# Early products by rows of x, other exact pairs, and a new order in an attention and two-layer MoE kernel

## The chip, the cores and the metric

One NeuronCore of a Trainium2 chip runs the whole program. The metric is the device time of one launch in microseconds (us); a kernel's time is the median of its runs. The engines are TensorE (PE, its weight loads PEld), VectorE (DVE), ScalarE (ACT), GpSimd (POOL) and SyncE (SP), which here issues the DMAs.

## The reference, cut to what is computed

```python
# attention: q, k, v are (4, 8, 576, 64)
scores = softmax(causal(q @ k.T / 8))          # a /= a.sum(-1) + 1e-9
local = scores @ v
q_p = where(q > 0, q, exp(q) - 1) + 1          # phi
mem_out = (q_p @ M_prev) / (q_p @ z_prev + 1e-6)
x = g * mem_out + (1 - g) * local              # g = sigmoid(beta), per head
# x as 2304 tokens x 512
y = (silu(x @ w_gate) * (x @ w_val)) @ w_out   # 1536 hidden columns
h = y @ w_in                                   # 2048 hidden columns
out = where(h >= 1, h, where(h <= -1, 0, (h + 1) ** 2 / 4)) @ w_out2
```

## The kernel before

**Tiling.** The 32 heads are worked as 16 pairs (4 batches of 4 pairs), pairs 0 to 15 in this text. x stands transposed in DRAM (xs): its 512 columns are four rows of 128, and pair n of a batch writes row n for that batch's 576 tokens. A matmul operand is held as a high and a low part, and a product of two such operands is three matmuls (high by low, low by high, high by high). ScalarE makes the high part (a cast, `split`, "name.hi"), VectorE the low part (a difference, "name.lo"); for v and x the difference is GpSimd's. Some pairs instead multiply in plain fp32 from one copied operand ("exact"), which takes TensorE longer and leaves out the low parts: pairs below EXACT (8) for the last product av (probabilities R by v), below EXACT_Q (2) for the scores s (tiles K and SZ), below EXACT_M (4) for the memory product. In a pair with split scores the parts of K for the second head reach the other half of the partitions by a DMA ("dup", K onto K).

**One pair.** q, k, v are loaded by SP; TensorE transposes k and q; scores s; VectorE takes mask, scale and row minimum (a, mn); ScalarE takes the Exp with the row sum; VectorE turns sums into factors (`scales`, with `over`: one scalar_tensor_tensor and one reciprocal); GpSimd scales the rows of a; TensorE transposes them; copies or splits give R; av ends the pair. Beside it phi goes min (VectorE), Exp (ScalarE), p (VectorE), the norm (GpSimd and VectorE), its transposes PP, and enters av by M. A pair with split operands joins av's two halves (ScalarE copy avt, VectorE sum xf), casts x (`x_hi`), takes the difference (`x_lo`) and stores the row (`x_out`).

**Early products.** While attention runs, twelve weight units (gate and val of the first six hidden tiles) are decoded, and for the token groups 0 to 511, 512 to 1023 and 1024 to 1535 the products with them are done as soon as all their batches are stored (`early_unit`): four rows of x are loaded as xh (`load_x`, four buffers), each unit takes 12 matmuls of 512 columns in one PSUM bank of the three called mm, cut into two halves of two rows (CUTS), then ScalarE copies the bank to gvo and SP stores it to gv. A second stage then loads xb, the same four rows for groups of tokens, first the two groups of batch 3 (384 tokens each), does their gate and val products, decodes more weights (raw to wA and wS to wu on VectorE), and goes on with the rest of the first layer and the second layer.

**What sets the order.** A planner (`Plan`) takes tasks with an engine, a cost, a priority and their dependences, plays them through as a list scheduler, and writes each engine's instructions in the order that comes out; the engines run theirs in order. The priority of an attention task is a number for its pair plus an entry of the table ORDER; EARLY holds those of the twelve weight units, GROUP_AT those of the early products of batches 0 to 2, X_AT those of their xh loads. In the second stage each xb group is loaded at priority 22 plus its number, the first weights are decoded at -20.

## Time and profile before

| | before |
|---|---|
| median of 3 runs | 1140.66 us (1140.23 to 1140.68) |
| the profiled execution | 1140.29 us |
| its span in the trace | 1138.2 us |
| TensorE busy | 1092.1 us, 96% |
| VectorE busy | 752.9 us, 66% |
| ScalarE busy | 551.9 us, 48% |
| GpSimd busy | 234.4 us, 21% |

The profiled execution is one more run of the kernel; its span reaches from its first to its last recorded instruction, and 2.1 us of its time lie around the span. Busy times are those of instructions recorded on an engine; waits, semaphores and DMA issues are not counted as busy. A share over the whole span mixes attention (the first 377 us) with the two layers behind it, so the rows further below are cut by stretches.

### The profile page before, as it was taken

The page shows a single profiled execution, that of the slowest core. Times are in us where ns is not written, and L with a number is a line of the kernel's source. Part 1 is how long each engine was busy: PE and PEld are TensorE (multiplying, and loading weights), DVE is VectorE, ACT ScalarE, POOL GpSimd, SP SyncE. Part 2 cuts the span into 40 slices and gives each one's busy share as a digit, 9 for nine tenths or more (in the row PEclk, how much of TensorE's full clock was granted, in tenths as well). Part 3 has the DMA queues.
Part 4 walks back from the last instruction along what each step waited for, and adds up shares of the span by engine and source line. Part 5 has one row for each costly group of instructions (what it writes and reads, how often), then busy time and mean ns, then how long its engine had stood idle before and what let it go on. Part 6 is the DMA issues. An engine that isn't in the chain of part 4 may idle for free.

```text
span 1138.2 us, 16428 instructions
## 1 busy us (share of the span) xinstructions
PE 1092.1 (96%) x5544; PEld 928.9 (82%) x5544; DVE 752.9 (66%) x1698; ACT 551.9 (48%) x1258; POOL 234.4 (21%) x314
## 2 busy tenths in 40 slices
PE   6688999999999699999999999999999999999998
PEld 4455677888888699888889998888888888899997
DVE  5567977788886487799954458999634343343433
ACT  6568886888896144455433334444222222222222
POOL 5568677458464000000000000000000000000000
PEclk9889999999999899999999999999999999999999
DMA  5545854665632878987545466562210110010000
GB/s 120 145 115 140 241 136 139 188 172 157 197 104 87 286 224 292 349 330 243 165 135 168 126 238 203 169 238 93 70 37 1 44 50 1 24 55 1 28 1 28
DMA packets 148644, 157.59 MB, mean 138 GB/s; under 512 B 70224, under 2 KB 109136, under 8 KB 148560
## 3 DMA queue, kind: packets, MB, share of 16 engines
q1 hardware_dynamic: 148560, 156.54, 44.1%
q8 instruction: 44, 0.72, 0.3%
q14 instruction: 40, 0.33, 0.1%
HBM read 105.78 MB, written 42.47 MB: 130 GB/s over the span
## 4 chain that ended last, share of the span: by engine, by line
PE 74%; DVE 8%; ACT 7%; DMA 4%; issue 3%; POOL 2%; SPq 1%; ACTq 0%; POOLq 0%; DVEq 0%
PE mm L1015 37%; PE acc L1245 26%; PE av L842 5%; ACT a L663 2%; PE s L650 1%; PE t L781 1%; DMA KK<-KK 1%; DMA raw<-in_moe_w_val_dram 1%; PE s L684 1%; DVE t L1209 1%; DVE wA L956 1%; DVE h L1222 1%; DVE t L1215 1%; ACT KK L380 1%; DMA raw<-in_moe_w_out_dram 1%
## 5 line engine op out<-in xcount | busy, mean ns | idle before, releaser
L1015 PE MATMUL mm<-xb,wu 128*128 128x512 f32 (+1 forms) x1968 | 413.2, 365 | 9.0 <-DMA xb<-xs 9.0
L1015 PEld LDWEIGHTS mm<-xb,wu 128*128 128x128 f32 x1968 | 359.6, 189 | 51.6 <-issue 9.4
L1245 PE MATMUL acc<-wu,h 128*128 128x512 f32 x864 | 208.1, 390 | 0.0
L1245 PEld LDWEIGHTS acc<-wu,h 128*128 128x128 f32 x864 | 161.7, 188 | 32.4
L1219 ACT CAST h<-t 128x512 fp32r<-128x512 f32 (+1 forms) x140 | 80.9, 578 | 185.4 <-DVE t L1213 90.0
L1245 PE MATMUL acc<-h,wu 128*128 128x512 f32 (+1 forms) x720 | 152.2, 368 | 1.5 <-DVE h L1222 1.4
L1207 DVE SCALAR_TENSOR_TENSOR t<-t 128x512 f32<-128x512 f32 (+1 forms) x80 | 51.0, 637 | 146.7 <-ACT t L1201 146.7
L1245 PEld LDWEIGHTS acc<-h,wu 128*128 128x128 f32 x720 | 131.0, 188 | 19.2 <-DVE h L1222 2.4
L1222 DVE TENSOR_TENSOR h<-t,h 128x512 fp32r<-128x512 f32 (+1 forms) x140 | 89.1, 636 | 79.3 <-ACT h L1219 78.9
L1201 ACT ACTIVATE t<-mm,half 128x512 f32<-128x512 f32 (+1 forms) x80 | 51.5, 644 | 147.4 <-PE mm L1015 147.1
L1015 PE MATMUL mm<-xh,wu 128*128 128x512 f32 x432 | 114.4, 404 | 0.0
L734 POOL TENSOR_SCALAR a<-a,sum 128x256 f32<-128x256 f32 (+3 forms) x144 | 85.8, 613 | 33.4 <-DVE sum L568 17.4
L1015 PEld LDWEIGHTS mm<-xh,wu 128*128 128x128 f32 x432 | 77.2, 189 | 14.4
L663 ACT ACTIVATE a<-a,mn 128x128 f32<-128x128 f32 (+3 forms) x128 | 71.3, 559 | 8.8 <-DVE mn L656 8.3
L1060 ACT COPY gvo<-mm 128x512 f32<-128x512 f32 (+1 forms) x80 | 43.2, 548 | 56.1 <-PE mm L1015 55.0
L656 DVE CUSTOM_DVE_ANT_0 a<-s,mask 128x128 f32<-128x128 f32 (+3 forms) x128 | 58.9, 482 | 12.8 <-PE s L650 9.8
L923 ACT ACTIVATE wA<-raw 128x512 f32<-128x512 f32 x64 | 43.1, 674 | 48.7 <-DVE wu L963 14.9
L960 ACT CAST wu<-wA 128x512 fp32r<-128x512 f32 x64 | 39.7, 620 | 47.8 <-DVE wA L956 45.7
L650 PE MATMUL s<-KK,SX 128*128 128x512 f32 (+3 forms) x224 | 50.1, 340 | 3.5 <-DMA KK<-KK 1.4
L1213 DVE TENSOR_TENSOR t<-t,mm 128x512 f32<-128x512 f32 (+1 forms) x80 | 50.6, 632 | 2.2
L842 PE MATMUL av<-R,vn 128*64 128x320 f32 (+4 forms) x224 | 51.4, 371 | 0.0
L842 PEld LDWEIGHTS av<-R,vn 128*64 128x64 f32 x224 | 30.5, 142 | 24.9 <-issue 6.4
(132 smaller groups left out, 1394.2 us busy)
## 6 DMA issues: line engine op xcount, KB each, us to landing
raw<-in_moe_w_out_dram SPq DMA_DIRECT2D x28, 512.0 KB, 5.4
gv<-gvo SPq DMA_DIRECT2D x48, 256.0 KB, 4.5
xb<-xs SPq DMA_DIRECT2D x24, 512.0 KB, 6.6
gv<-gv SPq DMA_DIRECT2D x24, 512.0 KB, 6.0
xs<-x SPq DMA_DIRECT2D x16, 576.0 KB, 3.0
raw<-in_moe_w_in_dram SPq DMA_DIRECT2D x16, 512.0 KB, 5.6
KK<-KK SPq DMA_DIRECT2D x28, 288.0 KB, 4.2
raw<-in_moe_w_gate_dram SPq DMA_DIRECT2D x12, 512.0 KB, 4.7
```

What stands on the lines that cost most here:

```text
L650: nc.tensor.matmul(s[:, 0:kl], st["S"][h][:, c * P:(c + 1) * P], st["K"][h][:, j, 0:kl], start=(j == 0), stop=(j == 1))
L656: nc.vector.tensor_tensor_reduce(a, st[f"s{h}{c}"][:, 0:kl], self.mask0[:, 512 - kl:512], -0.125, 3.0e38, ALU.add, ALU.min, mn[:, o:o + 1])
L663: nc.scalar.activation(a, a, AF.Exp, bias=mn[:, o:o + 1], scale=-1.0, accum_out=sm[:, o:o + 1])
L734: nc.gpsimd.tensor_scalar(a, a, r, 1.0, op0=ALU.mult, op1=ALU.mult)
L842: nc.tensor.matmul(o[0:m, c0:c1], l, r, start=(i == 0), stop=(i == len(mms) - 1), skip_group_check=True)
L1015: nc.tensor.matmul(out, kt_of(unit, pw, kt), x[kt][:, px, cols], start=(kt == 0 and i == 0), stop=(kt == KT - 1 and i == 2))
L1201: nc.scalar.activation(s["t"], src[0][0](), AF.Relu, bias=half, scale=0.5)
L1207: nc.vector.scalar_tensor_tensor(s["t"], s["t"], 1.0, s["t"], op0=ALU.min, op1=ALU.mult)
L1213: nc.vector.tensor_max(s["t"], s["t"], src[0][0]())
L1219: nc.scalar.copy(s["h"][:, 0], s["t"])
L1222: nc.vector.tensor_sub(s["h"][:, 1], s["t"], f32(s["h"][:, 0]))
L1245: nc.tensor.matmul(state[m][:, 0:o], l, r, start=(f == 0 and i == 0), stop=(f == F - 1 and i == 2), skip_group_check=True)
```

## The change

Nine things change.

1. **Exact pairs.** av is multiplied in fp32 for pairs 0 to 3 only (before 0 to 7); the scores for pairs 0 to 3 (before 0 and 1).
2. **Early products by rows.** A unit's 12 matmuls are cut into four quarters, one for each row of x, and a quarter depends on its own xh row alone (before on all four). An xh load depends on the store of its own row alone.
3. **min by ScalarE.** VectorE's min(q, 0) becomes ScalarE's Relu(-q), and the Exp behind it takes scale -1.
4. **Sums.** The row sums stand in the first column of a tile of two columns whose second column holds 1e-9; a reduction over the two replaces the scalar_tensor_tensor. 1/OGP (the factor of 1 - g) is worked out once, and GpSimd's scaling takes it as its second scalar in place of the constant 1.
5. **Own stores.** The gv stores of the last two hidden tiles of group 1024 to 1535 (four) are issued by ScalarE.
6. **xb loads first.** The first two groups of the second stage have their loads at priority -50 and -49, ahead of the weight decoding at -20.
7. to 9. ORDER, EARLY, GROUP_AT and X_AT have new numbers.

```diff
-EXACT = 8
-EXACT_Q = 2
+EXACT = 4
+EXACT_Q = 4
 EXACT_M = 4
...
-CUTS = (0, 2, 4)
-EARLY = (370, 1555, 928, 1016, 176, 628, 40, 285, 537, 6951, 2735, 393)
+CUTS = (0, 1, 2, 3, 4)
+EARLY = (-442.191, 1095.2181, 3514.6201, 5388.5521, -113.2042, 1597.6845, 2014.1923, 166.5095, 4349.2967, 5245.9815, 1051.2236, -130.0942)
 XH, GVO = 4, 3
+OWN = 2
...
-GROUP_AT, X_AT = (27859, 18087, 4829), (572, 439, -332)
+GROUP_AT, X_AT = (25118.8269, 36624.3422, 30122.3043), (360.7705, 632.4816, -116.8892)
...
 ORDER = {
-    "load": -667, "load_v": -340, "load_z": -340, "load_M": -296, "tk": 12, "tm": -870, "tk.hi": 1965, "tm.hi":
+    "load": -945.7389, "load_v": 592.0326, "load_z": -927.2927, "load_M": -295.3806, "tk": -367.2275, "tm":
...
+        nc.vector.reciprocal(self.OGP, self.OGP)
+
+        self.sum = [ac.tile([P, 9, 2], F32, name=f"sum_{i}") for i in range(3)]
+        for t in self.sum:
+            nc.gpsimd.memset(t[:, :, 1], 1e-9)
...
         def f_min():
             e = st["e"] = self.ph.tile([P, 9, D], F32, name="e", tag="e")
-            nc.vector.tensor_scalar(e, st["qn"], 0.0, None, op0=ALU.min)
+            nc.scalar.activation(e, st["qn"], AF.Relu, scale=-1.0)
 
         def f_exp():
-            nc.scalar.activation(st["e"], st["e"], AF.Exp)
+            nc.scalar.activation(st["e"], st["e"], AF.Exp, scale=-1.0)
...
-        t = add("DVE", c_dve(576), "min", f_min, [l_q], [i_q, i_e], True)
+        t = add("ACT", c_act(576) + 40, "min", f_min, [l_q], [i_q, i_e])
...
-                            "sum": self.sm.tile([P, 9], F32, name="sum", tag="sum")}
+                            "sum": self.sum[i_mn.slot],
+                            "r": self.sm.tile([P, 9], F32, name="r", tag="r")}
...
-                    nc.scalar.activation(a, a, AF.Exp, bias=mn[:, o:o + 1], scale=-1.0, accum_out=sm[:, o:o + 1])
+                    nc.scalar.activation(a, a, AF.Exp, bias=mn[:, o:o + 1], scale=-1.0, accum_out=sm[:, o, 0:1])
...
-            return over(lambda: mk_mn()[1][:, lo:hi], 1e-9, self.OGP[:, n, lo:hi], f"sum{h}",
-                        [t_exp[x] for x in keys], [i_mn])
+            def f_sum():
+                mk_mn()
+                nc.vector.tensor_reduce(st["mn"]["r"][:, lo:hi], st["mn"]["sum"][:, lo:hi], axis=AX.X, op=ALU.add)
+
+            def f_inv():
+                r = st["mn"]["r"][:, lo:hi]
+                nc.vector.reciprocal(r, r)
+
+            t = add("DVE", 80, f"sum{h}", f_sum, [t_exp[x] for x in keys], [i_mn])
+            return add("DVE", 94, f"sum{h}", f_inv, [t], [i_mn])
...
-                r = mk_mn()[1][:, o:o + 1]
-                nc.gpsimd.tensor_scalar(a, a, r, 1.0, op0=ALU.mult, op1=ALU.mult)
+                nc.gpsimd.tensor_scalar(a, a, st["mn"]["r"][:, o:o + 1], self.OGP[:, n, o:o + 1], op0=ALU.mult, op1=ALU.mult)
...
-    def early_unit(plan, mm, f, tok, x, pool, prio, tag, cap, deps=()):
+    def early_unit(plan, mm, f, tok, x, pool, prio, tag, cap, deps=(), own=False):
...
-                t = [plan.add("PE", cost, prio - (i > 0), lambda i=i, prod=prod: prod(i), t + [u["t"], *x["t"], *deps],
-                              [i_p, u["i"], *x["i"]])]
+                t = [plan.add("PE", cost, prio - (i > 0), lambda i=i, prod=prod: prod(i),
+                              t + [u["t"], *x["t"][CUTS[i]:CUTS[i + 1]], *deps],
+                              [i_p, u["i"], *x["i"][CUTS[i]:CUTS[i + 1]]])]
             t = plan.add("ACT", c_act(gt), prio - 1, copy, t, [i_p, i_o])
-            plan.dma(prio, [1.42 * gt], lambda j=j: nc.sync.dma_start(gv[f][:, j, tok], s["o", j]), [t], [i_o])
+            if own:
+                t = plan.add("ACT", 50, prio - 2, lambda j=j: nc.scalar.dma_start(gv[f][:, j, tok], s["o", j]), [t], [i_o])
+                plan.add("DMA", 1.42 * gt, prio, lambda: None, [t], [i_o])
+            else:
+                plan.dma(prio, [1.42 * gt], lambda j=j: nc.sync.dma_start(gv[f][:, j, tok], s["o", j]), [t], [i_o])
...
-            s["t"].append(plan.dma(prio, [n * 2.85], f, list(deps), [i_x], last))
+            s["t"].append(plan.dma(prio, [n * 2.85], f, list(deps[kt]) if deps else [], [i_x], last))
...
-                stored = [t for e in range(tok.start // S, b + 1) for t in t_x[e]]
+                stored = [[t_x[e][kt] for e in range(tok.start // S, b + 1)] for kt in range(KT)]
                 xh = load_x(plan, xs, fpool, "xh", tok, X_AT[b], stored)
                 for f in range(D0):
-                    early_unit(plan, mm, f, tok, xh, gpool, GROUP_AT[b], "gvo", "gvo")
+                    early_unit(plan, mm, f, tok, xh, gpool, GROUP_AT[b], "gvo", "gvo",
+                               own=b == B - 2 and f >= D0 - OWN)
...
-        xh = load_x(plan, xs, xb, "xb", tok, 22 + h)
+        xh = load_x(plan, xs, xb, "xb", tok, h - 50 if h < 2 else 22 + h)
```

What the order on the engines makes of it, at three places. First SP's queue where attention ends; xs_67 is x in DRAM, the stores x_5041 and x_4997, x_5105 are those of the last pairs, gvo the early results, raw the weights. Before:

```order
L883 DMA xs_67<-x_5041 128x2x576
L1068 DMA gv5_74<-gvo_5074 128x512
L918 DMA raw_5128<-in_moe_w_gate_dram 128x4x256
L1068 DMA gv5_74<-gvo_5077 128x512
L918 DMA raw_5130<-in_moe_w_val_dram 128x4x256
L918 DMA raw_5132<-in_moe_w_gate_dram 128x4x256
L1082 DMA xb_5134<-xs_67 128x2x384
L1082 DMA xb_5136<-xs_67 128x2x384
L1082 DMA xb_5138<-xs_67 128x2x384
L1082 DMA xb_5140<-xs_67 128x2x384
```

After, with the four rows of the first xb group as xb_5213, 5215, 5217 and 5219:

```order
L903 DMA xs_67<-x_4997 128x2x576
L1094 DMA gv3_72<-gvo_5039 128x512
L1109 DMA xb_5213<-xs_67 128x2x384
L1109 DMA xb_5215<-xs_67 128x2x384
L1094 DMA gv3_72<-gvo_5097 128x512
L903 DMA xs_67<-x_5105 128x2x576
L1109 DMA xb_5217<-xs_67 128x2x384
L1109 DMA xb_5219<-xs_67 128x2x384
L1109 DMA xb_5221<-xs_67 128x2x384
L1109 DMA xb_5223<-xs_67 128x2x384
L1109 DMA xb_5225<-xs_67 128x2x384
L1109 DMA xb_5227<-xs_67 128x2x384
```

The xb loads stood behind the last x store, three weight loads and two gv stores; now rows 0 and 1 stand ahead of the last x store, row 2 and row 3 right behind it, and the second group before any weight.

Second, TensorE's queue at the same place. Before, av01_5026 is the last attention product, xh the third group's rows, xb_5134 row 0 of the first group of the second stage:

```order
L842 MATMUL av01_5026<-R0_5010,vhl_4802 128x128
L1015 MATMUL mm_5016<-xh_4092,wu_2463 128x512 x3
L1015 MATMUL mm_5016<-xh_4101,wu_2463 128x512 x3
L1015 MATMUL mm_5043<-xh_4083,wu_2185 128x512 x3
L1015 MATMUL mm_5043<-xh_4085,wu_2185 128x512 x3
L1015 MATMUL mm_5054<-xh_4083,wu_1091 128x512 x3
L1015 MATMUL mm_5054<-xh_4085,wu_1091 128x512 x3
L1015 MATMUL mm_5043<-xh_4092,wu_2185 128x512 x3
L1015 MATMUL mm_5043<-xh_4101,wu_2185 128x512 x3
L1015 MATMUL mm_5054<-xh_4092,wu_1091 128x512 x3
L1015 MATMUL mm_5054<-xh_4101,wu_1091 128x512 x3
L1015 MATMUL mm_5173<-xb_5134,wu_982 128x384 x3
```

Between the last av and the first xb product stood ten rows of three matmuls. After, seventeen such rows on xh (51 matmuls) stand there, of which these are the last four, ahead of the first xb rows:

```order
L1035 MATMUL mm_5129<-xh_4272,wu_1042 128x512 x3
L1035 MATMUL mm_5136<-xh_4272,wu_647 128x512 x3
L1035 MATMUL mm_5129<-xh_4364,wu_1042 128x512 x3
L1035 MATMUL mm_5136<-xh_4364,wu_647 128x512 x3
L1035 MATMUL mm_5237<-xb_5213,wu_545 128x384 x3
L1035 MATMUL mm_5241<-xb_5213,wu_1206 128x384 x3
L1035 MATMUL mm_5237<-xb_5215,wu_545 128x384 x3
L1035 MATMUL mm_5241<-xb_5215,wu_1206 128x384 x3
L1035 MATMUL mm_5237<-xb_5217,wu_545 128x384 x3
L1035 MATMUL mm_5241<-xb_5217,wu_1206 128x384 x3
L1035 MATMUL mm_5237<-xb_5219,wu_545 128x384 x3
L1035 MATMUL mm_5241<-xb_5219,wu_1206 128x384 x3
```

The two units of the second stage now alternate by row of x, and row 3 (xb_5219) has 18 matmuls on rows 0 to 2 ahead of it.

Third, TensorE's queue where the first early products stand; xh_1455, 1468, 1473 and 1479 are rows 0 to 3 of the first group, before among the scores of pair 5:

```order
L650 MATMUL s12_1627<-KK_1306,SX_1421 128x384 x2
L1015 MATMUL mm_1638<-xh_1455,wu_982 128x512 x3
L1015 MATMUL mm_1638<-xh_1468,wu_982 128x512 x3
L781 MATMUL t03_1656<-ident_60,a3_1497 128x128 x4
L781 MATMUL t02_1662<-ident_60,a2_1512 128x128 x3
L650 MATMUL s11_1670<-KK_1306,SX_1421 128x256 x2
L650 MATMUL s10_1673<-KK_1306,SX_1421 128x128 x2
L520 MATMUL tq_1678<-ident_60,qn_1235 128x128 x4
L1015 MATMUL mm_1638<-xh_1473,wu_982 128x512 x3
L1015 MATMUL mm_1638<-xh_1479,wu_982 128x512 x3
```

After, among the scores of pair 3 (KK_785, in fp32), with xh_729 as row 0 of that group:

```order
L818 MATMUL t01_917<-ident_60,a0_673 128x128
L818 MATMUL t01_917<-ident_60,a1_669 128x128 x2
L1035 MATMUL mm_922<-xh_729,wu_545 128x512 x3
L659 MATMUL s12_934<-KK_785,SZ_1_179 128x384
L659 MATMUL s11_939<-KK_785,SZ_1_179 128x256
L659 MATMUL s10_946<-KK_785,SZ_1_179 128x128
L778 MATMUL t4_949<-ident_60,a4_0_170 128x128 x4
L780 MATMUL t5_954<-ident_60,a4_0_170 128x128
L487 MATMUL tm_961<-ident_60,kn_0_166 128x128
L489 MATMUL tm_961<-ident_60,qn_781 64x128
L1035 MATMUL mm_968<-xh_729,wu_764 128x512 x3
L482 MATMUL tk_978<-ident_60,kn_0_166 128x128 x4
```

The first row's products (of two units in these rows) stood behind pair 3's store and now begin in the middle of pair 3; in all 27 early matmuls (three units, rows 0 to 2) now stand ahead of the first one on row 3.

## Rows read from the trace of the kernel before

**Rows 1.** The table of stretches of the whole span: stretch, its length, then the busy time (and number of instructions) of PE, PEld, DVE, ACT and POOL, the granted clock of PE (1.00 is full), the DMA share and GB/s.

```profile
0.00:112.60 112.60, 87.46 (x424) 59.44 (x424) 71.11 (x226) 75.86 (x211) 74.45 (x108) 0.91 0.52 131
112.60:135.20 22.60, 18.81 (x110) 13.52 (x111) 20.12 (x61) 18.13 (x53) 14.62 (x20) 1.00 0.81 234
135.20:377.40 242.20, 240.09 (x1455) 203.42 (x1455) 189.09 (x565) 194.05 (x536) 145.37 (x188) 1.00 0.52 150
377.40:387.70 10.30, 1.35 (x6) 0.76 (x5) 4.18 (x10) 1.16 (x2) 0.00 (x0) 0.78 0.86 292
387.70:1138.20 750.50, 744.42 (x3552) 651.71 (x3552) 468.40 (x839) 262.73 (x459) 0.00 (x0) 1.00 0.39 131
```

**Rows 2.** The timeline from 362 to 396 us, where attention ends and the second stage begins: start, busy time, engine, line, operation, out<-in, count, and in brackets the idle time before it and what ended it.

```profile
371.13 0.57 PE L842 MATMUL av<-R,vhl 128*128 128x256 f32 x4
...
371.54 7.22 PE L1015 MATMUL mm<-xh,wu 128*128 128x512 f32 x30
...
374.85 0.37 SPq L883 DMA_DIRECT2D xs<-x  x1
...
381.03 6.93 SPq L1082 DMA_DIRECT2D xb<-xs  x9
382.80 0.43 DVE L925 TENSOR_SCALAR wA<-raw 128x512 uint32<-128x512 uint32 x1 [10.24 <-DMA raw<-in_moe_w_gate_dram]
...
387.72 8.58 PE L1015 MATMUL mm<-xb,wu 128*128 128x384 f32 x33 [8.97 <-DMA xb<-xs]
```

**Rows 3.** The timelines of TensorE from 109 to 140 us and, behind the second dots, of SP from 115 to 130 us; columns as in rows 2.

```profile
111.76 0.81 PE L842 MATMUL av<-R,vn 128*64 128x256 f32 x4
...
135.18 1.56 PE L1015 MATMUL mm<-xh,wu 128*128 128x512 f32 x6
...
116.57 0.37 SPq L883 DMA_DIRECT2D xs<-x  x1
...
118.58 1.85 SPq L423 DMA_DIRECT2D mraw<-in_M_prev_dram  x2
120.48 3.42 SPq L1082 DMA_DIRECT2D xh<-xs  x4
```

**Rows 4.** The table of stretches for the two stretches behind the handoff; columns as in rows 1.

```profile
387.70:395.00 7.30, 7.28 (x27) 7.12 (x28) 7.17 (x15) 0.71 (x2) 0.00 (x0) 0.61 1.06 374
395.00:400.00 5.00, 5.00 (x31) 5.00 (x30) 2.92 (x6) 1.79 (x4) 0.00 (x0) 1.00 1.07 378
```

**Rows 5.** The page's part on DMA issues: out<-in, engine, operation, count, KB each, and the median us from issue to landing.

```profile
xb<-xs SPq DMA_DIRECT2D x24, 512.0 KB, 6.6
...
xs<-x SPq DMA_DIRECT2D x16, 576.0 KB, 3.0
...
KK<-KK SPq DMA_DIRECT2D x28, 288.0 KB, 4.2
```

**Rows 6.** TensorE's timeline at 8 to 18 us (a pair with fp32 scores), at 109 to 140 us (pair 4) and at 362 to 396 us (pair 15); columns as in rows 2. A stretch of a head reaches from one row's start to the next one's.

```profile
10.51 4.77 PE L646 MATMUL s<-KK,SZ 128*128 128x512 f32 x16
15.12 0.60 PE L520 MATMUL tq<-ident,qn 128*128 128x128 f32 x4
...
124.10 1.50 PE L650 MATMUL s<-KK,SX 128*128 128x512 f32 x8
...
129.92 0.45 PE L842 MATMUL av<-PP,Mhl 128*64 128x256 f32 x2
...
133.73 0.73 PE L650 MATMUL s<-KK,SX 128*128 128x512 f32 x2
...
364.37 0.31 PE L842 MATMUL av<-PP,Mhl 128*128 128x320 f32 x1
...
366.37 0.36 PE L842 MATMUL av<-PP,Mhl 128*128 128x320 f32 x1
```

**Rows 7.** The groups of instructions with their shapes kept apart: line, engine, operation, out<-in, count, then busy time and the mean ns of one, then the idle time before them and what ended it.

```profile
L384 DVE TENSOR_TENSOR SX<-tq,SX 64x512 fp32r<-64x512 f32 x28 | 19.3, 688 | 9.7 <-ACT SX L380 9.1
L384 DVE TENSOR_TENSOR KK<-tk,KK 64x512 fp32r<-64x512 f32 x28 | 19.3, 688 | 5.4 <-ACT KK L380 5.0
...
L380 ACT CAST R<-t 128x384 fp32r<-128x384 f32 x32 | 15.3, 489 | 1.3 <-PE t L798 0.9
...
L542 ACT ACTIVATE e<-e 128x576 f32<-128x576 f32 x16 | 11.0, 690 | 2.4 <-DVE e L539 2.3
...
L384 DVE TENSOR_TENSOR R<-t,R 128x512 fp32r<-128x512 f32 x16 | 10.9, 683 | 1.0 <-ACT R L380 0.8
...
L539 DVE TENSOR_SCALAR e<-qn 128x576 f32<-128x576 f32 x16 | 8.4, 526 | 0.2 <-DMA qn<-in_q_dram 0.2
...
L617 ACT CAST vhl<-vn 128x640 fp32r<-128x640 f32 x8 | 5.8, 726 | 2.5 <-DMA vn<-in_v_dram 1.5 <-issue 1.0
...
L877 ACT CAST x<-xf 128x576 fp32r<-128x576 f32 x8 | 5.3, 668 | 0.6 <-DVE xf L854 0.5
...
L559 DVE TENSOR_REDUCE nrm<-e 128x9 f32<-128x144 f32 x16 | 4.8, 297 | 2.1 <-POOL e L562 2.0
...
L566 DVE SCALAR_TENSOR_TENSOR sum<-sum,OGP 128x5 f32<-128x5 f32 x16 | 3.6, 227 | 4.5 <-ACT a L663 2.5 <-ACT a L703 1.7
```

**Rows 8.** The table of stretches from 260 to 300 us; columns as in rows 1.

```profile
260.00:300.00 40.00, 39.89 (x254) 35.37 (x254) 35.86 (x106) 35.82 (x100) 31.08 (x39) 1.00 0.60 163
```

**Rows 9.** The chain of waits, of its pieces between 40 and 60 us: start, length, what.

```profile
49.48 3.04 DMA KK<-KK
```

More of the change, by code (lines that the diff above doesn't have):

```diff
@@ L58 @@
 ORDER = {
-    "load": -667, "load_v": -340, "load_z": -340, "load_M": -296, "tk": 12, "tm": -870, "tk.hi": 1965, "tm.hi":
-    2421, "tq": 368, "tq.hi": -564, "min": 376, "exp": 1667, "phi": 778, "w": 1073, "fold": -336, "nrm": -864,
[7 rows of a table removed]
-    "dup": -549, "tq.lo": -1, "M_hi": -179, "M_lo": 4881, "tp.lo": -458, "tp4.lo": 60, "v_hi": 862, "v_lo": 342,
[3 rows of a table removed]
+    "load": -945.7389, "load_v": 592.0326, "load_z": -927.2927, "load_M": -295.3806, "tk": -367.2275, "tm":
+    -578.2612, "tk.hi": 33.8866, "tm.hi": 2503.4172, "tq": 366.5828, "tq.hi": 551.7409, "min": 282.7648, "exp":
[9 rows of a table added]
+    573.6966, "av11.hi": 1003.8975, "av11.lo": -702.4225, "x_out": 495.0346, "M_hi": -1886.6655, "M_lo":
+    846.6585, "tk.lo": -1349.8413, "tm.lo": -148.6078, "dup": -152.5341, "tq.lo": 1465.0258, "tp.lo": 4629.9943,
[4 rows of a table added]
 }
@@ L702, in ex @@
                 mn, sm = mk_mn()
-                nc.scalar.activation(a, a, AF.Exp, bias=mn[:, 0:1], scale=-1.0, accum_out=sm[:, 0:1])
+                nc.scalar.activation(a, a, AF.Exp, bias=mn[:, 0:1], scale=-1.0, accum_out=sm[:, 0, 0:1])
             t_exp[4] = add("ACT", c_act(576) + 225, "ex4", ex, [t], [i_a[4], i_mn])
@@ L1295, in tile_attention_two_moe @@
         n = tok.stop - tok.start
-        y = load_x(plan, ys, xb, "xb", tok, base, t_y0 if tok.start == 0 else ally)
+        y = load_x(plan, ys, xb, "xb", tok, base, [t_y0 if tok.start == 0 else ally] * KT)
         state = {"cols": DM}
```

23 rows, old and new, of the table ORDER are left out of this document.

## The prediction, made blind

> **What bounds the kernel now.** I read first the table of stretches [rows 1]. It cuts the 1138.2 us span into five. In the first 112.6 us (pairs 0 to 3) TensorE is busy 87.46 us, and the reader should see that no other engine is near full either (71 to 76 us): this part is bound by waits from engine to engine. From 112.6 to 135.2, when the first early product starts, it is busy 18.81 of 22.60. From 135.2 to 377.4 it is busy 240.09 of 242.20: TensorE sets the pace, with ScalarE at 194.05 and VectorE at 189.09. Then it stands still for about 9 us at the handoff. From 387.7 to the end it is busy 744.42 of 750.50; this change touches almost nothing there. So there is something to gain in the first 135 us (idle), in the 242 us (work) and at the handoff.
>
> The second view is the timeline of the handoff [rows 2]. The last attention product ends at 371.70. The chain behind it in the code (ScalarE copy, VectorE sum, ScalarE cast, GpSimd difference) ends in the x store issued at 374.85. The first x load of the second stage is issued only at 381.03, after three weight loads and two stores on SP. TensorE, which has used up 30 early products that started at 371.54, starts again at 387.72, released by that load. The third view is the early timeline: the last av products of pair 3 start at 111.76, its x store goes out at 116.57, its xh loads at 120.48, the first early product starts at 135.18 [rows 3].
>
> **The change, part by part.** All terms are against the span of the profiled execution; 2.1 us lie around it (1140.29 against 1138.2), and it is 0.4 below the median of 1140.66.
>
> (c) *Handoff.* Removed: 8.97 us of idle [rows 2], and the half clock behind it: 27 products start in the 7.3 us after 387.7, at a granted 0.61, and 31 in 5.00 us once it is 1.00 [rows 4]. At the later rate 7.3 us hold 45, so 18 are missing, 18 x 0.161 = 2.9 us. Together 11.9. What is late next is row 3 of x (the last pair's). By the order on SP it is issued right behind the last x store: 3.15 us from the end of the last av product to that store (371.70 to 374.85), 3.0 to land, 0.4 for the issue, 6.6 for the load [rows 2, 5]: 13.2 us. By the order on TensorE that is covered by 51 early products at 0.24 us (30 took 7.22) and 18 of rows 0 to 2 at 0.161: 15.1 us. So it is hidden with 1.9 us to spare; if loads are slow, 1 to 3 us remain. I take -11, bounds -12 and -9. The weight loads now stand behind the eight x loads; the first product with a new weight stands 144 products (23 us) into the second stage, and VectorE decodes the first weight from 382.80 [rows 2]. That cover shrinks by about 11 us; if it is gone, up to 5 us are lost there. I take 0.
>
> (b) *135 to 377.* Pairs 4 to 7 no longer multiply in fp32. One head of pair 4 runs from 129.92 to 133.73, 3.81 us; a head with split operands from 364.37 to 366.37, 2.00 us [rows 6]. That is 1.81 x 2 heads x 4 pairs = -14.5; pair 4's heads lie before 135.2, so -10.9 here and -3.6 in (a). Also 27 early products (three units, three rows each; only three accumulators exist) stand in the new order before the last row of pair 3: -6.2 here, moved into (a). By TensorE alone the stretch would be 242.2 - 10.9 - 6.2 = 225.
>
> But ScalarE gets more. Each pair gets a Relu in place of VectorE's min: no row shows it, the nearest is the Exp of the same shape, 690 ns (VectorE's min took 526) [rows 7]; bounds 526 and 726, the cast of 640 columns. Each of pairs 4 to 7 adds two casts at 489, one of v at 726, one of x at 668 [rows 7]: 2.4 us. In this stretch that is 194.1 + 11 x 0.69 + 3 x 2.4 = 208.8 us. The highest share that ScalarE reaches beside a full TensorE is 35.82 of 40 us [rows 8]; at that share 208.8 us need 233. I take 232, so -10, bounds -17 (TensorE alone) and 0. VectorE: -11 x 0.526, and for each of pairs 5 to 7 eight lo parts of at most 683 [rows 7], + 3 x 5.5: 199.8 us, which at its 35.86 of 40 us [rows 8] need 223. GpSimd gets one difference of v and one of x a pair more and had 97 us of room [rows 1]. Neither binds. The sums: a scalar_tensor_tensor (227 ns on five columns) becomes a reduction of ten or eight numbers; the reduction of 144 numbers took 297 [rows 7]. It lies between -0.1 and +0.1 us, 32 times, on an engine with room: 0. GpSimd's scale reads two scalar columns instead of one and a constant: same form, 0. Four stores issued by ScalarE instead of SP, at up to 1.9 us for two of SP's, fall on the handoff, where ScalarE has room [rows 1, 3]: 0.
>
> (a) *Before 135.* Pair 4's -3.6. Pairs 2 and 3 now use fp32 for the scores: 4.61 us for both heads (10.51 to 15.12) against 2 x 1.50, +1.6 each [rows 6]; with the 6.2 us of moved products, 9.4 us of new TensorE work in a stretch that has 28.9 us idle. In return these pairs lose VectorE's lo parts (688 ns twice for k and twice for q) and the doubling DMA, which lands after 4.2 us and stands in the chain of waits with 3.04 [rows 5, 7, 9]. A third of the added work on the path (+3.1), one doubling off it (-3.0): about -4 with pair 4's. Bounds: -10 (3.8 more from filled idle and another 3 from pair 3), and +6 (all of the added work, no wait gone). Since the rest of the order of 16 pairs is new, the middle is a choice, and the range keeps both ends.
>
> Sum: -11 - 10 - 4 = -25; 1138.2 - 25 + 2.1 = 1115.3. The parts' ends give 1102 (-12 - 17 - 10 = -39) and 1137 (-9 + 0 + 6 = -3).
>
> **Rivals.** *ScalarE binds.* It runs in order, and an average of 90% over 230 us is what it has reached only for 40. If every microsecond that TensorE saves in (b) is spent waiting for copies, and (a) gives nothing, only the handoff is left: 1138.2 - 11 + 2.1 = 1129. For it: the waits of rows 1's full stretch are short and TensorE has no slack there. Against: at 35.82 of 40 us TensorE was still busy 39.89 [rows 8]. The Trainium skill speaks for this rival: "ScalarE: Activation LUTs", section "Rules for kernel authors", sends relu, max and min to VectorE, not ScalarE. The trace agrees on the price of one (526 against 690 ns).
>
> *TensorE binds everywhere*, ScalarE follows, and the loads of early x fill the idle: -17, -10, -11: 1102.
>
> *Slower: SP is held.* Each xh load now has its own wait for its pair's store, which lands 3.0 us after its issue [rows 5], and stands ahead of the next pairs' k and q loads and doublings on SP, in order. Twelve such loads instead of three groups of four: nine more holds, 27 us if each one delays a pair. With the handoff's -11 and (b) at -10 that is 1138.2 - 21 + 27 + 2.1 = 1146. It decides from seven holds on the path (21 us). Against: loads run a pair ahead, and the first 112 us have gaps on every engine.
>
> *The change doesn't do what it says*: with three accumulators held open, the early products wait for the last row as before, and what they took up on TensorE's queue delays scores. Then (a) is +6 and (b) loses its 6.2: 1131; it goes with the first rival.
>
> **How the numbers follow.** Forecast 1115: 0.60. ScalarE binds, or nothing gained early (1126 to 1137): 0.20. TensorE everywhere (1098 to 1104): 0.08. Slower, 1146: 0.09. Within 0.2% of 1140.66, which is about what a measurement of this kernel can tell from no change: 0.03, where the held SP just eats the gain. The range 1100 to 1137 leaves out the slower case, the tie and part of the fast one, less than 2 in 10. Faster 0.88, same 0.03, slower 0.09.
>
> **What would show it.** Handoff: no idle over 3 us in front of the first product that reads xb, and a granted clock of 1.00 there. (b): the stretch from the first product on the last row of x to the last xh product at about 232 us, with ScalarE at 90%; if TensorE shows idle released by ScalarE of over 10 us in it, the first rival holds. (a): the x store of pair 3 not later than at 117 us, and SP's waits on xs landings not in the chain. Wrong altogether: a second stage longer than 750 us by more than 5, or pair 3's store after 125.

## The result and the profile after

The changed kernel takes 1111.93 us (median of 4 runs, 1110.91 to 1116.19) against 1140.67 before (4 runs, 1140.23 to 1142.40): a ratio of 0.9752, 95% interval 0.9725 to 0.9780, or 28.7 us faster. The profiled execution took 1112.51 us with a span of 1110.7; before 1140.29 and 1138.2. The spans differ by 27.5 us; the forecast was 25.

The table of stretches of the changed kernel; columns as in rows 1.

```profile
0.00:361.31 361.31, 335.66 (x1969) 275.15 (x1969) 278.63 (x851) 303.24 (x826) 256.91 (x325) 0.98 0.57 158
361.31:1110.70 749.39, 741.70 (x3553) 649.28 (x3551) 470.18 (x848) 261.65 (x461) 0.00 (x0) 1.00 0.40 133
```

The cut is where the early products end: before at 378.76 (371.54 + 7.22 [rows 2]); in the changed kernel at 361.31, where the products on xb take over (the last early product, as modelled, ends 0.16 us later). So 17.45 us are gained ahead of the cut and 10.05 behind it (759.44 to 749.39). Ahead of it TensorE's busy time fell by 12.1 us (347.7 to 335.7) and its idle time by 5.4 (31.0 to 25.6).

The timeline of the handoff in the changed kernel; columns as in rows 2, to which these rows answer.

```profile
349.41 12.06 PE L1035 MATMUL mm<-xh,wu 128*128 128x512 f32 x51
...
353.13 0.36 SPq L903 DMA_DIRECT2D xs<-x  x1
353.58 6.19 SPq L1109 DMA_DIRECT2D xb<-xs  x6
...
361.31 13.85 PE L1035 MATMUL mm<-xb,wu 128*128 128x384 f32 x79
...
368.71 0.43 DVE L945 TENSOR_SCALAR wA<-raw 128x512 uint32<-128x512 uint32 x1 [17.86 <-DMA raw<-in_moe_w_gate_dram]
```

The reader is to see that the row on xb at 361.31 carries no bracket: the 8.97 us of idle [rows 2] are gone, and 51 early products fill 12.06 us. The weights are decoded 7.40 us behind the first product on xb, where before decoding stood 4.92 us ahead of it.

The table of stretches right there, to be read beside rows 4:

```profile
349.60:361.30 11.70, 11.70 (x51) 9.47 (x51) 0.76 (x2) 3.21 (x6) 1.43 (x1) 1.00 0.74 240
361.30:368.60 7.30, 7.30 (x44) 7.29 (x43) 0.00 (x0) 1.64 (x4) 0.00 (x0) 1.00 1.05 371
```

The granted clock is 1.00 and 7.3 us hold 44 products, before 27 at 0.61.

What TensorE waited for between its first early product (67.83 us) and the end of attention (the view of waits: what, for what; us in total, times, longest):

```profile
PE mm L1035 <- DMA xh<-xs: 3.6, 3, 2.7
PE s L663 <- DMA KK<-KK: 3.1, 3, 1.5
PE av L862 <- ACT R L392: 1.7, 1, 1.7
PE av L862 <- DVE KK L396: 1.0, 2, 0.5
PE t L818 <- ACT R L765: 0.9, 1, 0.9
PE t L780 <- ACT PP L504: 0.9, 1, 0.9
```

In the six longest entries two kinds of transfer end 6.7 us of it, ScalarE 3.5 (1.7 + 0.9 + 0.9).

### The profile page after: what moved, and what is told of

It reads as the page before. It is cut to its first block, busy times and chain, and to the rows that moved or that the text cites. A ratio compares the mean times of both kernels' runs of the same rounds, so it can differ in the third digit from the quotient of the medians.

```text
span 1110.7 us, 16486 instructions
## 1 busy us (share of the span) xinstructions
PE 1077.4 (97%) x5520; PEld 924.4 (83%) x5520; DVE 748.8 (67%) x1699; ACT 564.9 (51%) x1286; POOL 256.9 (23%) x325
## 4 chain that ended last, share of the span: by engine, by line
PE 78%; ACT 6%; DVE 5%; DMA 4%; POOL 3%; issue 2%; SPq 1%; POOLq 0%; DVEq 0%; ACTq 0%
PE mm L1035 40%; PE acc L1273 30%; PE av L862 3%; ACT a L676 2%; DMA xh<-xs 2%; PE s L663 2%; POOL a L754 1%; DMA KK<-KK 1%; PE t L801 1%; PE s L659 1%; DVE R L396 1%; ACT KK L392 1%; PE s L697 1%; ACT R L392 0%; POOL wu L983 0%
## 5 line engine op out<-in xcount | busy, mean ns | idle before, releaser
L1035 PE MATMUL mm<-xh,wu 128*128 128x512 f32 x432 | 122.3, 410 | 3.6 <-DMA xh<-xs 3.6
L754 POOL TENSOR_SCALAR a<-a,r,OGP 128x512 f32<-128x512 f32 (+3 forms) x144 | 96.5, 683 | 25.6 <-DVE r L745 12.0
L676 ACT ACTIVATE a<-a,mn 128x256 f32<-128x256 f32 (+3 forms) x128 | 71.3, 560 | 8.5 <-DVE mn L669 8.2
L669 DVE CUSTOM_DVE_ANT_0 a<-s,mask 128x256 f32<-128x256 f32 (+3 forms) x128 | 58.0, 485 | 14.0 <-PE s L663 10.6
L396 DVE TENSOR_TENSOR R<-t,R 128x384 fp32r<-128x384 f32 (+3 forms) x120 | 52.9, 482 | 8.0 <-ACT R L392 7.6
L955 DVE SCALAR_TENSOR_TENSOR wA<-raw,wA 128x512 uint32<-128x512 uint32 x68 | 49.1, 726 | 0.8
L862 PEld LDWEIGHTS av<-R,vhl 128*128 128x128 f32 x336 | 48.6, 193 | 0.5
```

The source lines that it names most:

```text
L396: nc.vector.tensor_sub(lo(), src(), f32(hi()))
L669: nc.vector.tensor_tensor_reduce(a, st[f"s{h}{c}"][:, 0:kl], self.mask0[:, 512 - kl:512], -0.125, 3.0e38, ALU.add, ALU.min, mn[:, o:o + 1])
L676: nc.scalar.activation(a, a, AF.Exp, bias=mn[:, o:o + 1], scale=-1.0, accum_out=sm[:, o, 0:1])
L754: nc.gpsimd.tensor_scalar(a, a, st["mn"]["r"][:, o:o + 1], self.OGP[:, n, o:o + 1], op0=ALU.mult, op1=ALU.mult)
L862: nc.tensor.matmul(o[0:m, c0:c1], l, r, start=(i == 0), stop=(i == len(mms) - 1), skip_group_check=True)
L1035: nc.tensor.matmul(out, kt_of(unit, pw, kt), x[kt][:, px, cols], start=(kt == 0 and i == 0), stop=(kt == KT - 1 and i == 2))
```

## The experiments

Twelve kernels ran beside the kernel before, whose median was 1140.63 to 1141.24 in the three sets. The times of a kernel spread by 1 to 13 us between runs, so the places are read from each profiled execution. "Ahead" is the time to the end of the last early product, "behind" the rest of the span; idle and granted clock are TensorE's ahead of the cut. r2, m2 and z1 keep the order and so the same 1969 matmuls ahead of the cut as the changed kernel; where TensorE is busy longer there (ahead less idle), the same work takes longer.

| kernel | median us | ahead us | idle us | clock | behind us |
|---|---|---|---|---|---|
| before | 1140.67 | 378.8 | 31.0 | 0.97 | 759.4 |
| changed | 1111.93 | 361.3 | 25.6 | 0.98 | 749.4 |
| h1, before with xb first | 1131.36 | 374.8 | 30.7 | 0.99 | 753.7 |
| h2, h1 with rows in stage 2 | 1133.78 | 379.7 | 32.1 | 0.97 | 753.1 |
| h3, changed with xb late | 1121.04 | 364.8 | 27.1 | 0.98 | 755.0 |
| r1, changed without rows | 1139.74 | 388.0 | 43.0 | 0.96 | 750.9 |
| r2, rows held back, same order | 1117.03 | 368.0 | 28.5 | 0.97 | 749.4 |
| x1, av in fp32 for 8 pairs | 1122.72 | 371.5 | 25.7 | 0.99 | 749.0 |
| x2, scores in fp32 for 2 pairs | 1140.03 | 386.1 | 45.2 | 0.96 | 750.3 |
| m1, min on VectorE, new plan | 1132.34 | 380.7 | 38.6 | 0.97 | 752.1 |
| m2, min on VectorE, same order | 1116.65 | 365.8 | 28.0 | 0.98 | 749.5 |
| n1, old numbers | 1129.55 | 377.1 | 39.2 | 1.00 | 749.1 |
| z1, old sums and stores, same order | 1114.26 | 363.1 | 24.3 | 0.97 | 749.4 |
| w1, one gap filled | 1110.41 | 358.1 | 24.2 | 1.00 | 749.7 |

### The handoff: h1, h2, h3

h1, on the kernel before:

```diff
-        xh = load_x(plan, xs, xb, "xb", tok, 22 + h)
+        xh = load_x(plan, xs, xb, "xb", tok, h - 50 if h < 2 else 22 + h)
```

> The kernel before with one edit: the first two groups of x in the second stage are loaded ahead of the weights (part 6 alone). Theory (the handoff needs three things together: loads first, products by rows, and enough early products behind the last attention product): only 30 early products stand behind it, 7.2 us, and the first product still waits for row 3 of x, whose load stands behind one store of an early result; that one is issued at about 378, lands some 7 us later, so TensorE starts at about 385 instead of 387.7: 2 to 4 us faster than before, with 5 to 7 us of idle left and the half clock behind it. Rival (the order of the loads is the handoff's whole loss): 9 to 12 us faster than before.

Measured: 1131.36 us (ratio 0.9922, 0.9891 to 0.9952), 9.6 us faster than the kernel before in its set (1140.95). The theory fell by its number; the rival's 9 to 12 came in the total. The timeline of h1:

```profile
374.82 0.36 SPq L1082 DMA_DIRECT2D xb<-xs  x1
374.82 2.77 PE L1015 MATMUL mm<-xb,wu 128*128 128x384 f32 x15
...
378.97 13.30 PE L1015 MATMUL mm<-xb,wu 128*128 128x384 f32 x75 [1.37 <-DMA xb<-xs]
```

TensorE goes on with products on xb at 374.82, while row 3's load is only being issued; it lands in 4.15 us, not 7. So the planner's dependence on all four rows only sets the order, and an instruction waits for the rows that it reads. 1.37 us of idle remain. Of the 9.6 us, only 5.8 stand behind the cut; the other part is ahead of it, where nothing was edited (374.8 against 378.8 us, with a granted clock of 0.99 against 0.97). So the order of the loads alone is not worth the rival's 9 to 12 us at the handoff.

h2 has the edit of h1 and, in the second stage alone, quarters in place of halves:

```diff
-                t = [plan.add("PE", cost, prio - (i > 0), lambda i=i, prod=prod: prod(i), t + [u["t"], *x["t"], *deps],
+                t = [plan.add("PE", cost, prio - (i > 0), lambda i=i, prod=prod: prod(i), t + [u["t"], *(x["t"][cuts[i]:cuts[i + 1]] if tag == "yo" else x["t"]), *deps],
```

> The kernel before with two edits: the loads of x first, and the products of the second stage (these alone) cut by rows of x, each quarter waiting for its own row. Theory: 12 products on rows 0 and 1 follow the 30 early ones at once, row 2 lands at about 382, row 3 at about 385; 3 to 5 us of idle are left in place of 8.97, in two pieces: 4 to 8 us faster than before. Rival (loads first alone are enough): the same as with the loads first alone, 9 to 12 us faster. Second rival (the products by rows give nothing): 2 to 4 us faster, as the theory has it for the loads alone.

Measured: 1133.78 us (0.9935, 0.9915 to 0.9956), 7.2 us faster than the kernel before in its set, which is the theory's number; 6.3 us of it stand behind the cut, against h1's 5.8. The idle in front of xb is 0.22 us and not the theory's 3 to 5. In front of row 3 stands this in h2's timeline:

```profile
379.66 3.30 PE L1015 MATMUL mm<-xb,wu 128*128 128x384 f32 x18
383.17 13.80 PE L1015 MATMUL mm<-xb,wu 128*128 128x384 f32 x78 [0.22 <-DMA xb<-xs]
...
408.14 12.08 PE L1015 MATMUL mm<-xb,wu 128*128 128x384 f32 x68 [2.08 <-ACT gvo L1060]
```

The rows take 1.15 us more idle away (18 products ahead of row 3 instead of 15), but later waits for ScalarE's copies of results give back about half of it.

h3, on the changed kernel:

```diff
-        xh = load_x(plan, xs, xb, "xb", tok, h - 50 if h < 2 else 22 + h)
+        xh = load_x(plan, xs, xb, "xb", tok, 22 + h)
```

> The changed kernel with the loads of x at their old place, behind three weight loads. Theory: the 51 early products cover 12 us by themselves; the first row of x is issued some 1.5 us behind the last store of x instead of ahead of it and shares the transfers with 1.5 MB of weights, so it lands 1 to 5 us after TensorE needs it: 1 to 6 us slower than the changed kernel. Rival (the order of the loads is the handoff's whole gain): 9 to 12 us slower. The forecast's term of 11 us for the handoff is divided by this run: what is not lost here is owed to the 51 products.

Measured: 1121.04 us (0.9827, 0.9799 to 0.9854), 9.1 us slower than the changed kernel, between both claims; 5.6 of it stand behind the cut. The timeline of h3:

```profile
356.43 0.37 SPq L903 DMA_DIRECT2D xs<-x  x1
...
359.18 11.11 SPq L1109 DMA_DIRECT2D xb<-xs  x9
367.52 2.34 PE L1035 MATMUL mm<-xb,wu 128*128 128x384 f32 x12 [2.75 <-DMA xb<-xs]
370.74 1.32 PE L1035 MATMUL mm<-xb,wu 128*128 128x384 f32 x6 [0.87 <-DMA xb<-xs]
```

Three weights put 2.4 us between the store and the first load, and 51 products don't cover the rest. So of the 10.05 us behind the cut, the place of the loads carries some 5.6, and the larger cover by early products (with the rows) the other 4.4; h1's 5.8, from the other side, agrees.

### Products by rows: r1, r2

r1 undoes part 2 in the changed kernel:

```diff
-CUTS = (0, 1, 2, 3, 4)
+CUTS = (0, 2, 4)
...
-                              t + [u["t"], *x["t"][CUTS[i]:CUTS[i + 1]], *deps],
+                              t + [u["t"], *x["t"], *deps],
...
-                stored = [[t_x[e][kt] for e in range(tok.start // S, b + 1)] for kt in range(KT)]
+                stored = [[t for e in range(tok.start // S, b + 1) for t in t_x[e]]] * KT
```

> The changed kernel with the products of x in halves of two rows that wait for all four rows, and with each load of x waiting for all four stores of its batch (part 2 undone, the numbers of the new order kept). Theory (27 early products fill idle of TensorE in the middle of pairs 3 and 4, and row 3 is hidden at the handoff): the early ones move back behind the store of pair 3, 6.2 us of idle come back, and 1 to 2 us at the handoff: 5 to 10 us slower than the changed kernel. Rival (with three accumulators the early products gain nothing, and twelve single loads of x hold SP): the same or up to 5 us faster.

Measured: 1139.74 us (0.9990, 0.9964 to 1.0016), 27.8 us slower, beyond every claim. Idle ahead of the cut is 43.0 us, and in SP's timeline of r1 two loads of v take 8.08 us from 105.57 on, with all that is queued behind them. The planner had made another order of everything. This run therefore says little of the rows; r2 keeps every engine's order and only holds the 27 matmuls back:

```diff
+        late = [t for t in out if t.get("row", 3) < 3]
+        if late:
+            first = next(t for t in out if t.get("row") == 3)
+            k = out.index(first)
+            early = [t for t in out[:k] if t in late]
+            out = [t for t in out[:k] if t not in late] + early + out[k:]
```

> The changed kernel with the 27 matmuls of the first token group on rows 0 to 2 held back until just ahead of the first one on row 3, and nothing else moved. It prices the early products by rows at the first group alone. Forecast's term: 27 matmuls, 6.2 us of idle in pairs 2 to 4 come back: 4 to 8 us slower than the changed kernel. Rival (they delayed the scores as much as they filled): within 2 us. Second rival (the 28 us of the run without rows are this): 15 us slower or more.

Measured: 1117.03 us, 5.1 slower than the changed kernel (span 6.7). The table of stretches of r2, and under it that of the changed kernel, cut where r2 starts its first early product:

```profile
0.00:114.04 114.04, 95.68 (x483) 64.80 (x483) 83.46 (x260) 91.66 (x253) 92.93 (x125) 0.97 0.61 160
114.04:367.99 253.95, 243.81 (x1490) 213.45 (x1489) 196.64 (x592) 211.14 (x574) 163.34 (x201) 0.97 0.54 153
```

```profile
0.00:114.04 114.04, 99.25 (x494) 68.27 (x494) 79.85 (x251) 90.01 (x247) 91.10 (x123) 0.96 0.60 158
114.04:361.31 247.27, 236.42 (x1476) 206.89 (x1476) 198.78 (x601) 213.23 (x581) 165.81 (x202) 0.99 0.55 158
```

In the first 114 us r2 leaves TensorE 3.6 us less busy, and the three other engines get 1.7 to 3.6 us further, so the early matmuls did cost the attention something there; behind that r2 needs 6.7 us more. Not all of it is waits: ahead of the cut the same matmuls take 3.8 us longer (339.5 busy against 335.7, at a clock of 0.97 against 0.98), and 2.8 us are idle (28.5 against 25.6). The intervals of the two ratios overlap (0.9767 to 0.9828 and 0.9725 to 0.9780). So the early products by rows are worth some 3 to 7 us here; the rival of 15 falls, and the one of 2 is not far.

### Exact pairs: x1, x2

x1 has `EXACT = 8` in the changed kernel, x2 has `EXACT_Q = 2`.

> The changed kernel with av in fp32 for pairs 0 to 7, as before (the scores of pairs 0 to 3 stay in fp32). Theory (TensorE sets the pace of the middle stretch, and the fp32 products are paid in full): four pairs take 14.5 us more of TensorE; ScalarE loses 4 x 2.4 us of casts, which gives back up to 7 of the idle that the changed kernel has there (11.0 us between its first early product and the second stage): 7 to 14 us slower than the changed kernel. Rival (ScalarE binds that stretch, so TensorE's work there is free): within 4 us of the changed kernel.

> The changed kernel with fp32 scores for pairs 0 and 1 alone, as before. Theory (fp32 scores of pairs 2 and 3 cost TensorE 3.2 us and pay by taking lo parts and a doubling DMA out of the way): the doubling is back in the chain twice, the gaps in the first 107 us grow: 0 to 6 us slower. Rival (the doubling is hidden, TensorE's 3.2 us count): 1 to 4 us faster.

x1 measured 1122.72 us (0.9845, 0.9825 to 0.9865), 10.8 slower: the theory's range, and outside the rival's 4. The plan is a new one here too, but idle is the same (25.7 against 25.6), so the difference is work. The stretch ahead of the cut in x1, beside the first line of the changed kernel's table above:

```profile
0.00:371.49 371.49, 345.75 (x1984) 273.87 (x1985) 270.46 (x824) 294.92 (x810) 245.07 (x317) 0.99 0.57 161
```

The av products alone, by the table of stretches for their line, x1 and then the changed kernel (stretch, length, PE and PEld busy, clock, DMA share, GB/s):

```profile
0.00:400.00 400.00, 96.63 (x544) 70.50 (x544) 0.99 0.58 164
```

```profile
0.00:400.00 400.00, 85.91 (x528) 72.06 (x528) 0.98 0.60 171
```

Four pairs cost 10.7 us, 2.68 each. ScalarE has 8.3 us less to do in x1 (294.9 against 303.2 us), which bought no idle back.

x2 measured 1140.03 us (0.9990, 0.9973 to 1.0007), 28.1 slower, beyond both claims: idle ahead of the cut is 45.2 us. As in r1 the plan was another one, and what fp32 scores are worth in time stays open. Their work on TensorE can be read: the score products take 85.88 us ahead of the cut in the changed kernel and 83.24 in x2, so 2.6 us more for two pairs (forecast 3.2).

### The min: m1, m2

m1 puts min on VectorE and tells the planner; m2 makes the same edit of the two instructions and leaves the planner's task with ScalarE, so TensorE's, GpSimd's and SP's orders stay.

```diff
-            nc.scalar.activation(e, st["qn"], AF.Relu, scale=-1.0)
+            nc.vector.tensor_scalar(e, st["qn"], 0.0, None, op0=ALU.min)
...
-            nc.scalar.activation(st["e"], st["e"], AF.Exp, scale=-1.0)
+            nc.scalar.activation(st["e"], st["e"], AF.Exp)
```

> The changed kernel with min(q, 0) on VectorE and a plain Exp, as before. Theory of the forecast (ScalarE at 90% of the middle stretch makes its 11 us of idle on TensorE, and the Relu is 7.6 us of that load): 1 to 5 us faster than the changed kernel, with TensorE's idle between the first early product and the second stage down from 11.0 us. Rival (the engines wait for each other's turn in the order and not for ScalarE's load): the same, or up to 4 us slower because the numbers of the order were not made for it.

> The changed kernel with min(q, 0) on VectorE and a plain Exp, and nothing else moved: the planner still books ScalarE for it, so TensorE's, GpSimd's and SP's orders are the changed kernel's word for word. It separates the price of the Relu from that of another order, which the run with the min on VectorE and a new plan mixed. Theory now (ScalarE's load is not what makes TensorE wait; the 20 us of that run were the order's): within 2 us of the changed kernel. Rival (the forecast's: ScalarE at 90% sets the stretch): 2 to 5 us faster. Second rival (VectorE is the dearer place, and the whole 20 us are the min's): 15 us slower or more.

m1: 1132.34 us (0.9922, 0.9896 to 0.9947), 20.4 slower than the changed kernel, beyond both claims. m2: 1116.65 us (0.9794, 0.9769 to 0.9820), 4.7 slower. So some 16 of m1's 20 us are the order's. The stretch ahead of the cut in m2:

```profile
0.00:365.83 365.83, 337.83 (x1969) 276.06 (x1969) 284.75 (x867) 295.28 (x810) 260.14 (x325) 0.98 0.56 156
```

ScalarE lost 8.0 us ahead of the cut in m2 (295.3 against 303.2), and idle rose from 25.6 to 28.0: the rival that ScalarE's load sets the stretch falls. The 4.7 us lie outside the theory's 2 as well; with VectorE 6.1 us busier (284.8 against 278.6) the min gains nothing there, and the price is far from 15 us. Its size is loose: the intervals of the two ratios overlap, and of the 4.5 us ahead of the cut 2.2 are the same matmuls taking longer and 2.4 are idle.

### The numbers: n1

n1 has the old ORDER, EARLY, GROUP_AT and X_AT in the changed kernel.

> The changed kernel with the old ORDER, EARLY, GROUP_AT and X_AT (parts 1 to 6 stay). Theory (the parts carry the gain: less work on TensorE, products by rows, loads first): it keeps the handoff and most of the saved work, 1112 to 1125 us. Rival (the numbers carry it, since the list scheduler's order with the old ones is made for another set of tasks): 1126 us or more, with the idle of the first 135 us as large as before, about 29 us, or larger.

Measured: 1129.55 us (0.9907, 0.9881 to 0.9933). The stretch ahead of the cut:

```profile
0.00:377.06 377.06, 337.83 (x1969) 270.91 (x1969) 284.65 (x851) 304.89 (x826) 257.42 (x325) 1.00 0.55 154
```

It has the full gain behind the cut (749.1) and nearly the whole saved work (TensorE busy 337.8 ahead of the cut, against 335.7), but 39.2 us of idle. The parts by themselves with the old numbers are worth 11.1 us of the 28.7, the numbers on top of them the other 17.6. What the new numbers are worth without the parts was not run; r1 and x2, which undo one part each under them, lose 28 us, which suggests that they fit this set of parts only, and the two can't be priced apart. The theory's range was missed by 4.6 us; the rival's time came, but not its idle: the first 135.2 us have 25.0 us, less than before, and the rest of the 39.2 stands behind them.

### What was costed at nothing: z1

z1 takes the old sums, the constant 1 in GpSimd's scaling and SP for the four stores, in the same order otherwise:

```diff
-                nc.vector.tensor_reduce(st["mn"]["r"][:, lo:hi], st["mn"]["sum"][:, lo:hi], axis=AX.X, op=ALU.add)
+                nc.vector.scalar_tensor_tensor(
+                    st["mn"]["r"][:, lo:hi], st["mn"]["sum"][:, lo:hi, 0], 1e-9, self.OGP[:, n, lo:hi], op0=ALU.add, op1=ALU.mult)
...
-                nc.gpsimd.tensor_scalar(a, a, st["mn"]["r"][:, o:o + 1], self.OGP[:, n, o:o + 1], op0=ALU.mult, op1=ALU.mult)
+                nc.gpsimd.tensor_scalar(a, a, st["mn"]["r"][:, o:o + 1], 1.0, op0=ALU.mult, op1=ALU.mult)
...
-            nc.scalar.dma_start(gv[f][:, j, tok], s["o", j])
+            nc.sync.dma_start(gv[f][:, j, tok], s["o", j])
```

> The changed kernel with the sums as before (scalar_tensor_tensor, GpSimd's scaling with one scalar column and the constant 1) and with the four own stores of ScalarE issued by SP at the same place, the plan unchanged otherwise. Forecast's terms: both are worth 0, so within 2 us of the changed kernel. Rival for the stores: on SP each waits for its copy ahead of the loads of x, so the handoff loses 1 to 4 us, to be seen as idle in front of the products on xb; rival for the sums: a gap of 0.1 us or more at each of the 32 factors, 3 us or more in the attention.

Measured: 1114.26 us (0.9769, 0.9735 to 0.9803), 2.3 above the changed kernel with overlapping runs (1111.48 to 1115.40 against 1110.91 to 1116.19). Behind the cut both take 749.4 us, so the stores are worth nothing here. Ahead of it z1 has 1.3 us less idle (24.3 against 25.6), while the same matmuls take 3.1 us longer (338.8 busy against 335.7, at a clock of 0.97 against 0.98). So the old sums bring no waits of 3 us or more, as the rival had it, and the 2.3 us by the medians are not shown to be theirs.

### The clock: w1

w1 adds transposes of the identity ahead of three waiting instructions of TensorE (3, 12 and 5 of them):

```diff
+        def filler(n):
+            t = mm.tile([P, HT], F32, name="mm", tag="mm0")
+            for _ in range(n):
+                nc.tensor.transpose(t[:, 0:P], ident, ident)
```

> The changed kernel with 20 more transposes of the identity (128 columns each, into a PSUM bank that is free then, read by nobody) on TensorE at 18 to 22 us, in the waits of 0.39, 1.66 and 0.81 us behind which its granted clock is 0.50 for some 6 us. Theory (the waits let the clock fall, and the half clock costs up to half of the 6.6 us): the clock stays at 1.00 between 20 and 30 us, and the span is 1 to 4 us shorter than the changed kernel's. Rival (the clock falls whatever TensorE does there, or falls later instead): the same, or longer by up to the 2.2 us that the added work takes.

Measured: 1110.41 us (0.9744, 0.9716 to 0.9772), 1.5 below the changed kernel with overlapping runs; span 2.9 shorter. The table of stretches of w1, then of the changed kernel:

```profile
22.00:30.00 8.00, 6.27 (x34) 4.42 (x35) 7.02 (x23) 7.92 (x27) 4.88 (x8) 1.00 0.53 138
```

```profile
22.00:30.00 8.00, 6.89 (x18) 4.24 (x18) 5.83 (x18) 7.09 (x26) 2.89 (x6) 0.58 0.57 149
```

The clock stays at full speed, as the theory has it, but the first early product starts at 68.52 us, not earlier than the 67.83 of the changed kernel; the time that the half clock took is idle instead (12.15 us up to there, against 11.28). The 2.9 us are gained later, where nothing was edited, and are no more than two runs of one kernel differ by. So the half clock in that place costs nothing that this run can show, and the theory's number came without its cause. w1 is the fastest median of all, but not by more than the noise.

## Why the prediction was right

The forecast was 1115 us, range 1100 to 1137; 1111.93 came. The likeliest case held: 27.5 us of span against a sum of 25. (The parts' fast ends, -39, give 1101.3 and not 1102.)

**(c) The handoff: right, the size nearly.** Forecast -11; 10.05 us behind the cut. Both parts came as worked out: 8.97 us of idle to none, and 17 more products in the same 7.3 us (forecast 18, which is 2.9 us). Row 3 was hidden by 51 + 18 products, as the order said. Some of it was given back: behind the first 12 us on xb TensorE's idle is 7.69 us, against 6.06 before, and the waits for VectorE's h in the second layer are 2.9 us, against 1.4. The weight loads, costed at 0, are not shown to be the cause, since h3, with the weights first again, has 3.6 us of those waits. h1 and h3 divide the term: 5.6 us for the loads' place, the rest for the longer cover.

**(a) and (b): right in sum, -17.45 against -14; the split between them and several sizes were off.** The forecast's mark between them is the first product on the last row of x in the first group: at 135.18 before, and now at 116.21, behind the 27 early ones. The tables of stretches up to the mark and from there to the cut, before and then after:

```profile
0.00:135.18 135.18, 106.25 (x533) 72.94 (x534) 91.22 (x286) 93.96 (x263) 89.05 (x127) 0.92 0.57 148
135.18:378.76 243.58, 241.46 (x1460) 204.19 (x1459) 189.11 (x565) 194.65 (x536) 145.39 (x188) 1.00 0.52 149
```

```profile
0.00:116.21 116.21, 101.30 (x510) 70.20 (x510) 82.02 (x260) 92.05 (x253) 93.04 (x125) 0.96 0.60 157
116.21:361.31 245.10, 234.37 (x1463) 204.95 (x1461) 196.61 (x592) 211.19 (x574) 163.87 (x201) 0.99 0.55 158
```

(a) gained 19.0 us where 4 were forecast, and (b), forecast at -10, came out 1.5 us longer. Part of this is attention work that moved across the mark (144 av products stand ahead of it, before 180). The gain is idle in (a), 28.9 to 14.9 us; in (b) TensorE's work fell by 7.1 us and its idle rose from 2.1 to 10.7. That the two misses nearly offset each other is luck. The sign named for (a) came: pair 3's x store goes out at 106.02 us, before at 116.57 [rows 3].

- The exact pairs were over-priced: 1.81 us a head, read from one head of each kind; x1 measures 1.34 on average (10.7 us over 8 heads), so 10.7 us in all instead of 14.5. The fp32 scores add 2.6 us (x2), so some 8 of the 12.1 us by which the busy time fell are work. Most of the rest agrees with a shorter time at half clock: by the granted clock of stretches of 5 us, TensorE was at 1.2 GHz for some 21 us ahead of the cut before (between 30 and 100 us) and some 14 in the changed kernel (20 to 30 and 105 to 130 us); these two are estimates, and 7 us less at half the rate are worth up to 3.5. The forecast had no term for that.
- The 27 early matmuls: -6.2 us in (b) against a third of that paid in (a), so about -4; r2 measured 5.1 by the medians, 2.8 of idle in the traces. Right in sign, the size loose.
- The idle in the middle, some 7 us by ScalarE's share: 10.7 us stand behind the mark, but from something else. ScalarE is busy 211.19 of 245.10 us there, 86%, near the 90% of the forecast; yet of the waits behind the mark it ends 1.7 us, where the forecast's sign for the first rival was over 10; m2 and x1, which take 8 us from it, have no less idle; and the longest waits are for xh rows (2.7 us) and for the doubling of K (3.1 us in three). This is the step that had the wrong mechanism: the number was near, the cause was not ScalarE's share.
- The Relu is 686 ns, the forecast's 690. The Trainium skill ("ScalarE: Activation LUTs", section "Rules for kernel authors") sends relu and min to VectorE, not ScalarE. The trace agrees on the price of one instruction (526 against 686 ns); m2, which does this for the min, is 4.7 us slower with overlapping intervals, so no gain of the rule shows in this order.
- The sums: the reductions take 155 and 156 ns, below the 227 (five columns) and 183 (four) of before, so inside the bound. GpSimd's scaling was mis-costed as "same form": with two scalar columns 512 elements take 787 ns, with one column and the constant in z1 708; over all shapes that is 14.7 us more on GpSimd. It was not quite free: TensorE's waits for GpSimd's a are 3.4 us in the changed kernel and 2.0 in z1.

The rows of the scaling, in the changed kernel and then in z1 (groups by shape, columns as in rows 7):

```profile
L754 POOL TENSOR_SCALAR a<-a,r,OGP 128x512 f32<-128x512 f32 x32 | 25.1, 787 | 9.5 <-DVE r L745 5.2 <-ACT SX L392 3.4 <-PE tp L593 0.9
...
L754 POOL TENSOR_SCALAR a<-a,r,OGP 128x128 f32<-128x128 f32 x32 | 17.9, 560 | 0.0
```

```profile
L754 POOL TENSOR_SCALAR a<-a,r 128x512 f32<-128x512 f32 x32 | 22.6, 708 | 10.8 <-DVE r L745 7.2 <-ACT SX L391 3.4
...
L754 POOL TENSOR_SCALAR a<-a,r 128x128 f32<-128x128 f32 x32 | 12.6, 395 | 0.0
```

**What the forecast left out** is a price for the new numbers of the order: on top of the parts they are worth 17.6 us by n1. It chose a middle between -10 and +6 for the first stretch and said so; the range held because of that, not because the order had been priced.

**The rivals.** ScalarE binds: refuted by x1 and m2. TensorE binds everywhere: not so either, 25.6 us of idle are left ahead of the cut. SP is held by single loads of x: in the changed kernel SP itself waits 5.6 us in four holds for stores of x up to 350 us, and all xh waits on TensorE's products are 3.6 us (2.7 the longest), far from the 27 that it needed. That the early products wait for the last row as before: refuted by the timeline, where one starts at 67.83 us, and by r2.
